# Loading, casting and transposing the first batch in two parts, with neighbouring heads paired and its keys evicted straight into blocks

## Chip, cores and metric

One core of one Trainium2 chip. The metric is the device time of one execution in microseconds, as the median of several runs. Engines: PE (TensorE, matrix products and transposes), DVE (VectorE), ACT (ScalarE), POOL (GpSimd), SP (issues most loads). In the profile L12 is line 12 of that kernel's source; line numbers differ from kernel to kernel.

## The reference

Sliding-window attention (8 batches, 8 heads, 576 positions, head size 64, window 32), followed by a two-layer network on all 4608 tokens.

```python
scores = scale * q @ k.T                        # (8, 8, 576, 576), kept where |i - j| <= 32
attn = softmax(scores)
x = (attn @ v).transpose(0, 2, 1, 3).reshape(4608, 512)
h = x @ w_in                                    # w_in 512 x 2048
out = np.maximum(0.01 * h, h) @ w_out           # w_out 2048 x 512, float32 out
```

## The kernel before

Heads are worked on in pairs, four to a batch. Each (batch, half of the sequence, pair) is one *attention step*: `score(i)` (five matmuls `ps`, exponential `e` on ACT, mask product `pr` on POOL) and `weighted(i)` (row sums `s`, weighted values `x`, reciprocal `r` and product `xT` on DVE). Four steps fill 288 rows of `xT`. These feed 16 *h tiles* (one h group), and every 128 rows of `gT` give one *output tile*.

```python
def load_qk(b, p, behind=None):
    for into, src, name in ((qf, q, "qf"), (kf, k, "kf")):
        t = fload.tile([96, 2, RUN * D], FP32, name=f"{name}{p}")
        if behind is not None:                      # the marker: a copy of 4 bytes that waits
            nc.sync.dma_start(out=t[0:1, 0, 0:1], in_=behind.bitcast(FP32))
            behind = None
        nc.sync.dma_start(out=t, in_=src[b, p:H:NPAIR].rearrange(...))   # heads p and p+4
...
# transposes(b): per pair q and k, 6 transposes each into one PSUM tile, then
nc.scalar.activation(out=kT_v, in_=tok, func=AF.Copy)
for a in range(2):
    nc.vector.tensor_copy(out=kbd[b % 2][r, p, :, r], in_=kT[r]...)      # keys into diagonal blocks
...
def o_tile(j, hook=None):
    o = mmps.tile([128, 512], FP32, name="mm", tag="mm")
    for f in range(FFC):
        if hook and f % 4 == 0:
            hook()                                  # steps that are due are put in here
        nc.tensor.matmul(o, gT[...], w_out_bf[:, f, :], ...)
    o_sb = outp.tile([128, DMODEL], FP32, name="o_sb")
    nc.scalar.activation(out=o_sb, in_=o, func=AF.Copy)
    nc.scalar.dma_start(out=out[ts(j, 128), :], in_=o_sb)
...
for i in range(NPAIR):                              # the start: steps 0 to 3
    score(i + 1)
    ...
    if i < 2: load_w_in(1024 + 512 * i, 1536 + 512 * i)
    else:     load_w_out(i - 2)
    weighted(i)
for p in range(NPAIR):                              # batch 1's q and k, behind a w_in chunk
    load_qk(1, p, w_in_bf[0:1, 0, 512:514] if p == 0 else None)
step(); load_w_out(2); load_w_out(3)
for f in range(FFC):                                # first h group, steps 5 to 7 in it
    h_tile(0, f)
    if f in (2, 6, 10): step()
    ...
for p in range(NPAIR):                              # batch 1's v, behind a w_out chunk
    load_v(1, p, w_out_bf[0:1, 4, 0:2] if p == 0 else None)
for f in range(FFC):                                # second h group, batch 1's transposes in it
    h_tile(1, f)
    if f % 4 == 3: next(second); next(second); ...
score(8)
# from here: output tiles with steps 8 to 11, third h group, and so on
```

The schedule is manual: each engine executes its instructions in the order written here.

The softmax here doesn't subtract the row's maximum and nothing guards it: scores larger than these inputs give would overflow.

## Time and profile before

| kernel before | us |
|---|---|
| time, median of 3 runs | 350.79 (350.40 to 351.71) |
| span of the profiled run | 349.3 |
| TensorE busy | 324.9 |
| first h tile starts | 28.91 |
| third h group starts | 70.37 |

The prediction below shows the lines of the start, the first h group and the first output tiles. Two more stretches complete the table of stages. The columns are the stretch, its length, busy time of PE, PEld, DVE, ACT and POOL with counts, granted clock, DMA share and GB/s.

```profile
41.55:52.25 10.70, 10.70 (x118) 8.49 (x116) 5.19 (x10) 9.73 (x24) 6.68 (x8) 1.00 0.91 193
70.37:349.30 278.93, 270.39 (x2285) 184.00 (x2301) 145.18 (x152) 162.27 (x355) 129.18 (x147) 1.00 0.34 96
```

The second h group has no idle PE time at all, and the rest of the kernel (279 us) is 97% busy.

### The profile page before, as it was taken

Reading aid. Unit: us, or ns where it says so; the run is one execution under the profiler, and the core shown is the slowest. Engines: PE = TensorE matmul, PEld = TensorE weight load, DVE = VectorE, ACT = ScalarE, POOL = GpSimd, SP = SyncE. Lnnn points to the kernel's source line nnn. Section 1 sums busy time; section 2 is a strip of 40 time slices with the busy share of each in tenths; the row PEclk is TensorE's granted clock in tenths of the full one; section 3 lists DMA queues with packets and bytes.
Section 4 is the critical chain, followed back from the end, with each engine's and each line's share of the span. In section 5 each row is a group of like instructions: output and inputs, shape, how many; then the busy total and the mean of one; then the engine's idle time right before and its main releaser. Section 6 shows DMA issues by size and latency. Waiting matters only on the chain.

```text
span 349.3 us, 6917 instructions
## 1 busy us (share of the span) xinstructions
PE 324.9 (93%) x2731; PEld 221.3 (63%) x2752; DVE 189.2 (54%) x206; ACT 203.8 (58%) x431; POOL 179.1 (51%) x213
## 2 busy tenths in 40 slices
PE   2558999998899999999999999999999999999995
PEld 1346775585675767667675766667675766666652
DVE  5487833865446656466456656566356656555200
ACT  6763793385563856566564756567474756455441
POOL 7696767566745636555354636555264644222000
PEclk9999999999999999999999999999999999999999
DMA  8999989968754433543444433553301001010101
GB/s 185 208 197 227 269 174 240 261 135 228 168 137 130 134 98 107 142 149 69 127 130 136 134 84 100 145 169 70 111 19 62 30 2 62 0 63 0 62 17 73
DMA packets 60708, 42.39 MB, mean 121 GB/s; under 512 B 39684, under 2 KB 56068, under 8 KB 60676
## 3 DMA queue, kind: packets, MB, share of 16 engines
q1 hardware_dynamic: 51204, 28.32, 34.7%
q10 hardware_dynamic: 5184, 9.44, 7.4%
q0 software_dynamic: 4288, 4.20, 7.3%
q8 instruction: 21, 0.34, 0.4%
q14 instruction: 11, 0.09, 0.1%
HBM read 36.70 MB, written 9.44 MB: 132 GB/s over the span
## 4 chain that ended last, share of the span: by engine, by line
PE 82%; ACT 5%; DVE 3%; issue 2%; DMA 2%; SPq 2%; POOL 1%; ACTq 1%; DVEq 0%; POOLq 0%
PE mm L280 35%; PE mm L266 33%; PE x L247 4%; PE tp L188 3%; PE ps L221 3%; DVE r L253 2%; DMA kf<-in_k_dram 2%; PE s L239 2%; ACT o_sb L285 2%; PE s L240 2%; ACT gT L270 1%; SPq L81 1%; SPq L70 1%; ACTq L286 1%; ACT kT L202 1%
## 5 line engine op out<-in xcount | busy, mean ns | idle before, releaser
L253 DVE RECIPROCAL r<-s 128x288 f32<-128x288 f32 x64 | 125.3, 1958 | 92.2 <-PE s L240 91.9
L231 POOL TENSOR_TENSOR pr<-e,mask 128x544 bf16<-128x544 bf16 x64 | 77.7, 1214 | 130.5 <-ACT e L227 130.3
L266 PE MATMUL mm<-xT,w_in_bf 128*128 128x288 bf16 x1024 | 136.8, 288 | 1.5 <-ACT gT L270 1.5
L280 PE MATMUL mm<-w_out_bf,gT 128*128 128x512 bf16 x555 | 128.1, 379 | 1.1
L266 PEld LDWEIGHTS <-w_in_bf 128*128 128x128 bf16 x1024 | 98.8, 98 | 28.7 <-issue 3.2
L270 ACT ACTIVATE gT<-mm 128x288 bf16<-128x288 f32 x256 | 101.9, 413 | 23.0 <-PE mm L266 8.8
L280 PEld LDWEIGHTS <-gT 128*128 128x128 bf16 x576 | 55.3, 98 | 60.5
L285 ACT ACTIVATE o_sb<-mm 128x512 f32<-128x512 f32 x36 | 21.5, 597 | 85.6 <-PE mm L280 85.6
L227 ACT ACTIVATE e<-ps 128x544 bf16<-128x544 f32 x64 | 39.8, 622 | 24.1 <-PE ps L221 12.9
L205 DVE COPY kbd<-kT 64x576 bf16<-64x576 bf16 x64 | 28.4, 444 | 32.4 <-ACT kT L202 32.0
L176 POOL CAST vbd<-vf 64x576 bf16<-64x576 f32 x58 | 38.4, 661 | 2.3 <-DMA vf<-in_v_dram 0.4
L255 DVE TENSOR_TENSOR xT<-x,r 128x288 bf16<-128x288 f32 x64 | 29.3, 458 | 6.7
L166 POOL CAST kb<-kf 96x768 bf16<-96x768 f32 x32 | 26.7, 837 | 8.1 <-DMA kf<-in_k_dram 8.1
L221 PE MATMUL ps<-qT,kbd 128*128 128x128 bf16 (+2 forms) x320 | 27.6, 220 | 0.0
L247 PE MATMUL x<-pr,vbd 128*128 128x128 bf16 (+2 forms) x320 | 27.1, 218 | 0.4 <-DVE xT L255 0.2
L221 PEld LDWEIGHTS <-kbd 128*128 128x128 bf16 x320 | 21.3, 103 | 7.2
L247 PEld LDWEIGHTS <-vbd 128*128 128x128 bf16 x320 | 21.8, 102 | 4.7 <-issue 1.9
L202 ACT ACTIVATE kT<-tp 128x576 bf16<-128x576 bf16 x32 | 20.8, 651 | 4.6 <-PE tp L188 2.8
L239 PE MATMUL s<-pr,ones_bd 128*128 128x288 bf16 x64 | 19.1, 298 | 4.7 <-DVE r L253 3.3
L196 ACT ACTIVATE qT<-tp 128x576 bf16<-128x576 bf16 x32 | 20.7, 648 | 3.9 <-PE tp L188 3.1
L188 PE MATMUL tp<-ident,qb 96*128 96x96 bf16 x192 | 14.4, 214 | 8.2 <-DVE qb L166 6.4
L166 POOL CAST qb<-qf 96x768 bf16<-96x768 f32 x24 | 19.7, 819 | 0.0
(31 smaller groups left out, 107.8 us busy)
## 6 DMA issues: line engine op xcount, KB each, us to landing
qf<-in_q_dram SPq DMA_DIRECT2D x32, 288.0 KB, 3.8
kf<-in_k_dram SPq DMA_DIRECT2D x32, 288.0 KB, 4.1
vf<-in_v_dram SPq DMA_DIRECT2D x64, 144.0 KB, 3.7
out_dram<-o_sb ACTq DMA_DIRECT2D x36, 256.0 KB, 2.3
w_in_bf<-in_moe_w_in_dram POOLq DMA_DIRECT2D x8, 256.0 KB, 6.4
w_out_bf<-in_moe_w_out_dram POOLq DMA_DIRECT2D x4, 512.0 KB, 12.8
qf<-w_in_bf SPq DMA_DIRECT2D x1, 0.0 KB
vf<-w_out_bf SPq DMA_DIRECT2D x1, 0.0 KB
```

The source lines that it names most:

```text
L166: eng.tensor_copy(out=dst[:, p], in_=src[b, p].rearrange("p a (c d) -> p c a d", d=D),)
L176: nc.gpsimd.tensor_copy(out=vbd[b % 2][r, p, :, r], in_=vf[b, p][r])
L221: nc.tensor.matmul(ps[:, c0:c0 + n], kbd[b % 2][:, p, blk], qT[b][:, p, q0:q0 + n], start=True, stop=True,)
L227: nc.scalar.activation(out=e, in_=ps[:, 512 - HALF:512 - HALF + NCOL], func=AF.Exp, scale=scale,)
L231: nc.gpsimd.tensor_mul(pr, e, mask[hf])
L247: nc.tensor.matmul(x[:, a:a + n], vbd[b % 2][:, p, blk, :], pr[:, c0:c0 + n], start=(n_ == 0), stop=(n_ == len(WIN[hf]) - 1), skip_group_c ...
L253: nc.vector.reciprocal(r, s)
L255: nc.vector.tensor_mul(xT[:, p, t0:t0 + HALF], x, r)
L266: nc.tensor.matmul(h[:, 0:HALF], w_in_bf[:, c, ts(f, 128)], xT[:, c, ds(t0, HALF)], start=(c == 0), stop=(c == DMC - 1),)
L270: nc.scalar.activation(out=gT[:, f, ds(t0, HALF)], in_=h[:, 0:HALF], func=AF.Prelu, alpha=0.01,)
L280: nc.tensor.matmul(o, gT[:, f, ds(128 * j % RING, 128)], w_out_bf[:, f, :], start=(f == 0), stop=(f == FFC - 1),)
L285: nc.scalar.activation(out=o_sb, in_=o, func=AF.Copy)
```

## The change

It is meant to shorten the start. Batch 0's q, k and v arrive in two parts by sequence, so that steps 0 to 3, which need only the first half of the queries, can begin before the rest is loaded, cast and transposed. Heads 2p and 2p+1 are paired in place of p and p+4, so a pair lies together in memory. Batch 0's keys go from PSUM straight into the blocks, without the DVE copies. To make room, other work moves: the second parts' casts and transposes and steps 4 to 7 into the first h group, two tiles apart; w_out's loads behind step 7; batch 1's loads behind w_out; batch 1's transposes and score 8 into the output tiles.

```diff
-                out=t, in_=src[b, p:H:NPAIR].rearrange("a (p c) d -> p a (c d)", c=RUN),
+                out=t, in_=src[b, 2 * p:2 * p + 2].rearrange("a (p c) d -> p a (c d)", c=RUN),
...
+    PART_Q = ((0, 3), (HALF, 3))
+    PART_K = ((0, 4), (384, 2))
+    PART_V = ((0, 5), (5, NB))
...        (load_qk0, load_v0, cast_qk0, cast_v0, transposes0: the same work for one part)
+                        kbd[0][r, p, t0 // 64:t0 // 64 + 96 * run // 64, r].rearrange(
+                            "p n (i c) -> p n i c", c=run),
+                        in_=tp[r].rearrange("p c (n i) -> p n i c", i=64 // run), func=AF.Copy,
...
-    for p in range(NPAIR):
-        load_qk(1, p, w_in_bf[0:1, 0, 512:514] if p == 0 else None)
-    step()
-    load_w_out(2)
-    load_w_out(3)
+    transposes0(0, 1)
+    score(4)
+    cast_v0(0, 1)
     for f in range(FFC):
         h_tile(0, f)
-        if f in (2, 6, 10):
-            step()
+        if f % 2 == 1:
+            i = (f - 1) // 2
+            if i < 3:
+                cast_qk0(i + 1, 1)
+                cast_v0(i + 1, 1)
+                transposes0(i + 1, 1)
+            if 1 <= i < 5:
+                step()
+            if i >= 4:
+                load_w_out(i - 4)
...
+        load_qk(1, p, w_out_bf[0:1, 4, 0:2] if p == 0 else None)
...
+    def step1():
+        i = state["done"]
+        if i == 8:
+            cast_v(1, 0)
+            score(8)
+        if i < 11:
+            cast_v(1, i - 7, on_act=i % 2 == 0)
+        load_v(2, i - 8)
+        step()
+    due += [(O_US * (3.9 + 2 * p), transposes1) for p in range(NPAIR)]
+    due += [(O_US * (8.9 + 1.6 * p), step1) for p in range(NPAIR)]
```

More of the change, by code (lines that the diff above doesn't have):

```diff
@@ L82, in load_v, with columns, load_qk0, load_v0 @@
                 out=t[64 * a:64 * a + 64],
-                in_=v[b, NPAIR * a + p].rearrange("(c p) d -> p c d", p=64),
+                in_=v[b, 2 * p + a].rearrange("(c p) d -> p c d", p=64),
             )
         vf[b, p] = t
-    load_qk(0, 0)
-    load_qk(0, 1)
-    load_v(0, 0)
-    load_qk(0, 2)
-    load_v(0, 1)
-    load_qk(0, 3)
-    load_v(0, 2)
-    load_v(0, 3)
+    PART_Q = ((0, 3), (HALF, 3))
+    PART_K = ((0, 4), (384, 2))
+    PART_V = ((0, 5), (5, NB))
+    for p in range(NPAIR):
+        qf[0, p] = fload.tile([96, 2, RUN * D], FP32, name=f"qf{p}")
+        kf[0, p] = fload.tile([96, 2, RUN * D], FP32, name=f"kf{p}")
+        vf[0, p] = fload.tile([128, NB, D], FP32, name=f"vf{p}")
+    def columns(part):
+        t0, run = part
+        return t0 // 96, t0 // 96 + run
+    def load_qk0(p, h):
+        for t, src, part in ((qf[0, p], q, PART_Q[h]), (kf[0, p], k, PART_K[h])):
+            t0, run = part
+            c0, c1 = columns(part)
+            nc.sync.dma_start(
+                out=t[:, :, c0 * D:c1 * D],
+                in_=src[0, 2 * p:2 * p + 2, t0:t0 + 96 * run].rearrange(
+                    "a (p c) d -> p a (c d)", c=run),
+            )
+    def load_v0(p, h):
+        n0, n1 = PART_V[h]
+        for a in range(2):
+            nc.sync.dma_start(
+                out=vf[0, p][64 * a:64 * a + 64, n0:n1],
+                in_=v[0, 2 * p + a, 64 * n0:64 * n1].rearrange("(c p) d -> p c d", p=64),
+            )
+    for p in range(NPAIR + 1):
+        if p < NPAIR:
+            load_qk0(p, 0)
+        if p > 0:
+            load_v0(p - 1, 0)
+    for p in range(NPAIR):
+        load_qk0(p, 1)
+        load_v0(p, 1)
     ident_f = const.tile([128, 128], FP32)
@@ L120, in clear @@
         )
-    nc.vector.memset(kbd[0], 0.0)
-    clear(vbd[0], 0)
-    clear(vbd[0], 1)
+    nc.vector.memset(kbd[0][:, 0:2], 0.0)
+    for p in range(3):
+        clear(vbd[0], p)
     WIN = [
@@ L147, with make_mask @@
     mask = [const.tile([128, NCOL], BF16, name=f"mask{i}") for i in range(2)]
-    def make_masks():
-        for hf in range(2):
-            lo = W * (hf + 1)
-            nc.gpsimd.tensor_copy(out=mask[hf][:, 0:HALF], in_=win_f[:, lo:lo + HALF])
-            nc.gpsimd.tensor_copy(out=mask[hf][:, HALF:NCOL], in_=win_f[:, 0:NCOL - HALF])
+    def make_mask(hf):
+        lo = W * (hf + 1)
+        nc.gpsimd.tensor_copy(out=mask[hf][:, 0:HALF], in_=win_f[:, lo:lo + HALF])
+        nc.gpsimd.tensor_copy(out=mask[hf][:, HALF:NCOL], in_=win_f[:, 0:NCOL - HALF])
     RING = 4 * HALF
@@ L176, in cast_v, with cast_qk0, cast_v0, transposes0 @@
                 nc.gpsimd.tensor_copy(out=vbd[b % 2][r, p, :, r], in_=vf[b, p][r])
+    def cast_qk0(p, h):
+        for eng, src, dst, part in (
+            (nc.vector, qf, qb, PART_Q[h]), (nc.gpsimd, kf, kb, PART_K[h]),
+        ):
+            c0, c1 = columns(part)
+            eng.tensor_copy(
+                out=dst[:, p, c0:c1],
+                in_=src[0, p][:, :, c0 * D:c1 * D].rearrange("p a (c d) -> p c a d", d=D),
+            )
+    def cast_v0(p, h, on_act=False):
+        n0, n1 = PART_V[h]
+        for a in range(2):
+            r = slice(64 * a, 64 * a + 64)
+            to, src = vbd[0][r, p, n0:n1, r], vf[0, p][r, n0:n1]
+            if on_act:
+                nc.scalar.activation(out=to, in_=src, func=AF.Copy)
+            else:
+                nc.gpsimd.tensor_copy(out=to, in_=src)
+    def transposes0(p, h):
+        if 0 not in qT:
+            qT[0] = attn.tile([128, NPAIR, S], BF16, name="qT")
+        for src, part in ((qb, PART_Q[h]), (kb, PART_K[h])):
+            t0, run = part
+            c0, c1 = columns(part)
+            tp = mmps.tile([128, run, 96], BF16, name="tp0", tag="mm")
+            for c in range(run):
+                nc.tensor.transpose(
+                    tp[:, c], src[:, p, c0 + c].rearrange("p a d -> p (a d)"), ident[0:96, 0:96],
+                )
+            if src is qb:
+                nc.scalar.activation(
+                    out=qT[0][:, p, t0:t0 + 96 * run].rearrange("p (i c) -> p i c", c=run),
+                    in_=tp.rearrange("p c i -> p i c"), func=AF.Copy,
+                )
+            else:
+                for a in range(2):
+                    r = slice(64 * a, 64 * a + 64)
+                    nc.scalar.activation(
+                        out=kbd[0][r, p, t0 // 64:t0 // 64 + 96 * run // 64, r].rearrange(
+                            "p n (i c) -> p n i c", c=run),
+                        in_=tp[r].rearrange("p c (n i) -> p n i c", i=64 // run), func=AF.Copy,
+                    )
     def transposes(b, first=False):
@@ L333, in step, with load_w_in @@
         state["done"] += 1
-    w_in_r = moe_w_in.rearrange("(a u d) f -> a d u f", a=2, d=D)
+    w_in_r = moe_w_in.rearrange("(u r) f -> r u f", r=128)
     w_out_r = moe_w_out.rearrange("(c p) f -> p c f", p=128)
-    def load_w_in(f0, f1):
-        for a in range(2):
-            nc.gpsimd.dma_start(
-                out=w_in_bf[64 * a:64 * a + 64, :, f0:f1], in_=w_in_r[a, :, :, f0:f1],
-            )
+    def load_w_in(i):
+        f = slice(512 * i, 512 * i + 512)
+        nc.gpsimd.dma_start(out=w_in_bf[:, :, f], in_=w_in_r[:, :, f])
     def load_w_out(i):
@@ L347, in load_w_out @@
         nc.gpsimd.dma_start(out=w_out_bf[:, c, :], in_=w_out_r[:, c, :])
-    first = transposes(0, first=True)
-    def first_pair():
-        next(first)
-        next(first)
-    cast_qk(0, 0, nc.vector)
-    make_masks()
-    cast_qk(0, 1, nc.vector)
-    first_pair()
-    first_pair()
-    clear(vbd[0], 2)
-    cast_v(0, 0)
-    cast_qk(0, 2, nc.vector)
-    score(0)
-    load_w_in(0, 512)
-    first_pair()
-    clear(vbd[0], 3)
-    cast_qk(0, 3, nc.vector)
-    load_w_in(512, 1024)
-    for i in range(NPAIR):
-        score(i + 1)
-        if i + 1 < NPAIR:
-            cast_v(0, i + 1, on_act=True)
-        if i < 2:
-            load_w_in(1024 + 512 * i, 1536 + 512 * i)
-        else:
-            load_w_out(i - 2)
-        weighted(i)
-        if i == 0:
-            first_pair()
@@ L380 @@
-    state["done"] = NPAIR
-    for p in range(NPAIR):
-        load_qk(1, p, w_in_bf[0:1, 0, 512:514] if p == 0 else None)
-    step()
-    load_w_out(2)
-    load_w_out(3)
+    cast_qk0(0, 0)
+    make_mask(0)
+    nc.vector.memset(kbd[0][:, 2:4], 0.0)
+    cast_qk0(1, 0)
+    nc.vector.memset(vbd[0][:, 3], 0.0)
+    transposes0(0, 0)
+    transposes0(1, 0)
+    cast_v0(0, 0)
+    cast_qk0(2, 0)
+    score(0)
+    transposes0(2, 0)
+    score(1)
+    cast_v0(1, 0, on_act=True)
+    cast_qk0(3, 0)
@@ L389 @@
+    weighted(0)
+    load_w_in(0)
+    transposes0(3, 0)
+    score(2)
+    cast_v0(2, 0, on_act=True)
+    weighted(1)
+    load_w_in(1)
+    score(3)
+    cast_v0(3, 0, on_act=True)
+    make_mask(1)
+    load_w_in(2)
+    weighted(2)
+    cast_qk0(0, 1)
+    load_w_in(3)
+    weighted(3)
+    state["done"] = NPAIR
+    transposes0(0, 1)
+    score(4)
+    cast_v0(0, 1)
     for f in range(FFC):
         h_tile(0, f)
-        if f in (2, 6, 10):
-            step()
-        if f % 4 == 3:
-            nc.gpsimd.memset(kbd[1][:, f // 4], 0.0)
+        if f % 2 == 1:
[8 more added lines that the diff above has]
+                load_w_out(i - 4)
@@ L395 @@
     for p in range(NPAIR):
-        cast_qk(1, p, nc.vector)
+        load_qk(1, p, w_out_bf[0:1, 4, 0:2] if p == 0 else None)
     for p in range(NPAIR):
-        load_v(1, p, w_out_bf[0:1, 4, 0:2] if p == 0 else None)
-    second = transposes(1, first=True)
+        load_v(1, p)
     for f in range(FFC):
@@ L402 @@
         if f % 4 == 3:
-            next(second)
-            next(second)
+            nc.gpsimd.memset(kbd[1][:, f // 4], 0.0)
             nc.gpsimd.memset(vbd[1][:, f // 4], 0.0)
+    for p in range(NPAIR):
+        cast_qk(1, p, nc.vector)
+        load_qk(2, p)
+    second = transposes(1, first=True)
     state["tp"] = 16
-    score(8)
-    for p in range(NPAIR):
-        load_qk(2, p)
     H_US, O_US, LEAD = 4 * (HALF / 2400 + 2.5e-3), 4 * 0.216, 4.0
@@ L428, with transposes1 @@
     due = []
-    for i in range(8, NC):
-        prev = 0.9 * O_US * 4 if i < 12 else at[i // 4 - 1] - LEAD
-        due.append(prev + (at[i // 4] - LEAD + (1.2 if i < 12 else 0) - prev) * (i % 4 + 1) / 4)
+    for i in range(12, NC):
+        g = i // 4
+        due.append((at[g - 1] + (at[g] - at[g - 1]) * (i % 4 + 1) / 4 - LEAD, step))
+    def transposes1():
+        next(second)
+        next(second)
+    def step1():
[9 more added lines that the diff above has]
+    due += [(O_US * (8.9 + 1.6 * p), step1) for p in range(NPAIR)]
+    due.sort(key=lambda t: t[0])
     clock = 0.0
-    cast_v(1, 0)
-    load_v(2, 0)
     def spend(us):
         nonlocal clock
-        while due and due[0] <= clock:
-            due.pop(0)
-            i = state["done"]
-            if i < 11:
-                cast_v(1, i - 7)
-                load_v(2, i - 7)
-            step()
+        while due and due[0][0] <= clock:
+            due.pop(0)[1]()
         clock += us
```

## The prediction

> **What bounds the kernel now.** I read the page first (busy shares), then the busy times by stretch, then TensorE's timeline, the groups of instructions, the DMA view and the SyncE queue's timeline.
>
> ```profile
> PE 324.9 (93%) x2731; PEld 221.3 (63%) x2752; DVE 189.2 (54%) x206; ACT 203.8 (58%) x431; POOL 179.1 (51%) x213
> ```
> TensorE is busy for 324.9 of 349.3 us, so 24 us is all that a reordering can win. Where they lie is told by the stretches: before the first h tile (28.9), the first h group with attention steps 4 to 7 (to 41.55), the second (to 52.25), the first output tiles (to 70.37).
>
> ```profile
> 0.00:28.90 28.90, 13.43 (x113) 9.57 (x114) 18.27 (x27) 18.13 (x25) 23.17 (x38) 1.00 1.12 197
> 28.90:41.55 12.65, 12.50 (x99) 9.39 (x98) 9.79 (x9) 7.29 (x17) 8.62 (x9) 1.00 1.17 256
> 52.25:70.37 18.12, 17.86 (x127) 9.87 (x127) 10.76 (x11) 6.34 (x11) 11.41 (x14) 1.00 1.19 249
> ```
> The columns are length, busy PE, PEld, DVE, ACT, POOL, granted clock, DMA share, GB/s. TensorE is idle for 15.5 us of the first 28.9, and for only 0.15 and 0.26 us in the two others. So the change can win at the start alone, and in the later stages it can only lose. DMA is full in all three.
>
> ```profile
> 25.26 0.42 PE L239 MATMUL s<-pr,ones_bd 128*128 128x288 bf16 x1 [1.06 <-DVE r L253]
> 27.95 0.42 PE L239 MATMUL s<-pr,ones_bd 128*128 128x288 bf16 x1 [1.06 <-DVE r L253]
> 28.91 3.08 PE L266 MATMUL mm<-xT,w_in_bf 128*128 128x288 bf16 x12
> 33.15 2.45 PE L266 MATMUL mm<-xT,w_in_bf 128*128 128x288 bf16 x16
> ```
> The start ends in a chain of steps 2.69 us apart (25.26 to 27.95): each sum s waits for the reciprocal before it, as s and x have one buffer. Then come h tiles, 12 matmuls in 2.9 us (0.24 each) at first, later 16 in 2.2 (0.14).
>
> ```profile
> L253 DVE RECIPROCAL r<-s 128x288 f32<-128x288 f32 x64 | 125.3, 1958 | 92.2 <-PE s L240 91.9
> L231 POOL TENSOR_TENSOR pr<-e,mask 128x544 bf16<-128x544 bf16 x64 | 77.7, 1214 | 130.5 <-ACT e L227 130.3
> ```
> A step costs 1.96 us of reciprocal plus 0.46 of multiply on DVE, and 1.21 on POOL. I use both below.
>
> ```profile
> 23.03 0.72 SPq L68 DMA_DIRECT2D qf<-w_in_bf  x1
> 27.54 0.34 SPq L70 DMA_DIRECT2D qf<-in_q_dram  x1
> 38.24 0.62 SPq L79 DMA_DIRECT2D vf<-w_out_bf  x1
> 46.39 0.68 SPq L81 DMA_DIRECT2D vf<-in_v_dram  x1
> ```
> Batch 1's loads are held back by one-element marker copies, which wait for a weight chunk. From the first marker's issue to the next load passed 4.5 us. Batch 1's v was all in near 54-55, only 2 to 3 us after the first output tile.
>
> **What the Trainium skill says.** "TensorE: Matmul & The Clock Gate", What's actually happening: TensorE idles at 1.2 GHz and gets 2.4 after about 3.4 us of sustained work. The trace agrees: 0.24 us per 288-column matmul up to 33, then about 0.14, though the page's clock row says 1.00 throughout. An earlier start of h therefore runs its first 4 to 5 us at half rate as before. "DMA: Bandwidth & Descriptors", Specifications: at least 512 B is needed for line rate. The trace agrees: packets under 512 B (v alone, 48 to 52 us) moved at 196 GB/s, those of q and k (55 to 60) at 261. Halved q and k runs keep to 512 B or more. The same page, Queues, rings and completion order: each engine takes queues in turn, a packet at a time. That fits the marker's 4.5 us beside weight loads, though no view shows the turn itself.
>
> **Rates and durations.** From the DMA view by stretch: v 3141 packets in 4 us on 16 engines, 20 ns a packet; q and k 907 in 5 us, 88 ns; weights 1216 in 6 us, 79 ns. So w_in and w_out (2048 packets each) are 10.1 us each, batch 1's q and k (1536) 8.5, its v (4608) 5.9. ACT reads 576 columns in 0.65 us and 288 in 0.41, so I estimate 0.49 for 384 and 0.34 for 192. POOL's cast of 768 takes 0.82, so 0.55 for 512 and 0.30 for 256 (estimates).
>
> **The change, part by part.**
>
> 1. *Half loads.* By the same rates the first parts make about 2.3 us of DMA per pair, where whole pairs made 3.8. kb of pair 3 was cast at 16.63; its half should land near 11.5. Data then no longer holds the start.
>
> 2. *Straight eviction.* Eight DVE copies of 0.44 us go, and ACT makes two evictions of 0.49 where it had one of 0.65. So DVE is freed and ACT is level.
>
> 3. *The start, walked through the new order of each engine.* ACT clears three blocks to 5.6, evicts pair 0 to 7.1 and pair 1 to 8.5, then exp to 9.1. POOL casts k2 to 9.4, pr0 to 10.6, pr1 to 12.75 and, queued behind it, k3 to 13.3. Sums: s0 at 10.65; s1 at 14.4 (behind k3's transposes); s2 at 17.05 and s3 at 19.7, both behind the reciprocal. Then follow transposes of pair 0's second part and score 4 (22.95). First h tile at **23.0 against 28.9: 5.9 us won**.
>
> 4. *The first h group.* It takes 12.65 us now. New in it: 15 transposes (0.65 us at full rate, more while cold) and waits. TensorE waits about 0.6 us for k1's cast behind pr4 and v0's casts on POOL; 1.45 us for q3's cast, which DVE has in line behind the reciprocal and multiply of step 4; and 1.75 us in steps 6 and 7, as these stand 2 h tiles apart (1.1 us and 0.75 of attention) while a reciprocal and multiply need 2.5. Before, four tiles stood between steps. That is 3.8 us of waits, 1.5 of transposes, 1.2 more at half rate: 19.1 in place of 12.65. It ends near 42.1, against 41.55. **The 5.9 us are given back here.** DVE meanwhile idles from 22.5 to 29.6, for step 4 comes only after four h tiles.
>
> 5. *The second h group* loses batch 1's 48 transposes (2.0 us) and score 8 (0.24): 16 tiles of 0.553, to 50.95 against 52.25. This work only moves into the output tiles, which now hold 18.1 + 2.3 = 20.4. Without waits the third h group would start at 71.4, against 70.4.
>
> 6. *Batch 1's data.* w_out is now issued behind pr7 (37.2), no longer at 24.6; DMA has finished w_in near 31 and idles. First packets at about 39.5, second chunk landed near 45.3, marker, q and k issued near 50, v0 landed near 62. The last w_out chunk lands near 50.5, in time. Batch 1's transposes are ordered from 54 on, 2.2 us apart, as its k lands (54.3, then 2.1 apart): waits of about 1 us. Step 8 is reached near 61.6, but pr8 is in POOL's line behind v0's casts: 62.2 + 1.4 + 1.2 = 64.8. A wait of 3.2 us; then steps at the reciprocal's pace keep 1 us more. The third h group starts near 75.7, **5.3 us late**.
>
> After that both orders are the same and TensorE-bound (270.4 of the last 278.9 us busy). Walked result: 350.8 + 5.3 = 356.
>
> **The rivals.** *Rival A, the start's gain survives.* If the first h group runs with no new waits, the third group starts near 71.4 - 3.8 = 67.6, and if batch 1 also comes in time the kernel takes about 348. For it: fewer DVE copies, and transpose times that fit k's landing so well that they look tuned. Against: 2.5 us of DVE per step against 1.85 of work between. *Rival B, only the batch 1 wait is smaller.* The marker may take 2 us in place of 4.5, as less is queued; packets may start 1 us sooner. Then step 8 waits next to nothing and the result is about 352. *Rival C, transfers collide at the start:* w_in shares DMA with second parts, chunk 0 is issued at 13.3 and lands only near 22, so the first h tile has 1 us of margin; POOL being 2 us late would make it 358.
>
> **Range and chances.** My walk took the slow value for the marker (2.5 us spread) and for TensorE's clock (cold to 29; 1.2 us spread). Half of both, 1.9, comes off 356: **354 us**. Each stage of the walk may be off by 1 to 2 us and three add up, so 347 to 359.5. Faster by over 2% (under 343.8) needs the 5.9 us kept and one more: 5%. Slower by over 2% (over 357.8) needs the walk and some of rival C: 16%. Within 2%: 79%.
>
> **What would show it.** First h matmul near 23 (within 1.5 us); the stretch from there to the second h group 17 to 20 us long, with TensorE waiting for qb behind DVE and for r; w_out issued after 35, DMA share falling between 31 and 39; q and k of batch 1 issued near 50; step 8's sum waiting for pr; third h group at 73 to 76. After it nothing should change: the length from there to the end is 279 us in both. I am wrong if the h stage shows no waits for DVE, if batch 1's v lands before the steps ask for it, or if the later stages shift by more than 1 us.

## More of the kernel before

One more stretch, cut by time, is needed to compare DMA later:

```profile
30.00:40.00 10.00, 9.85 (x81) 7.43 (x80) 7.24 (x7) 6.04 (x14) 5.97 (x7) 1.00 1.16 260
```

## The result and the profile after

The changed kernel takes **360.5 us** (359.86 to 360.62, 4 runs) beside 350.7 for the kernel before: ratio 1.027, 95% interval 1.0247 to 1.0294, so slower. A ratio here is the mean time of one kernel's fast runs over that of the other's fast runs of the same rounds, so not quite the ratio of the medians quoted. Outputs are correct.

The busy times by stretch of the changed kernel, cut at the same events (start, first h tile, second h group, first output tile, third h group, end):

```profile
0.00:21.84 21.84, 10.81 (x86) 7.30 (x87) 14.83 (x20) 15.76 (x29) 16.08 (x30) 1.00 0.85 180
21.84:41.50 19.66, 14.64 (x125) 10.78 (x124) 11.43 (x12) 11.01 (x28) 13.97 (x22) 1.00 0.70 116
41.50:49.33 7.83, 7.83 (x67) 6.25 (x65) 0.00 (x0) 6.57 (x17) 5.97 (x6) 1.00 1.17 189
49.33:79.66 30.33, 24.63 (x180) 13.66 (x177) 15.60 (x21) 13.54 (x23) 11.91 (x13) 0.89 1.01 215
79.66:358.80 279.14, 271.44 (x2307) 184.13 (x2303) 145.02 (x152) 162.65 (x355) 129.34 (x147) 1.00 0.37 101
```

| stage | before, us | after, us | difference | predicted for after |
|---|---|---|---|---|
| start | 28.91 | 21.84 | -7.07 | 23.0 |
| first h group | 12.64 | 19.66 | +7.02 | 19.1 |
| second h group | 10.70 | 7.83 | -2.87 | 8.85 |
| first output tiles | 18.12 | 30.33 | +12.21 | 24.75 |
| rest | 278.93 | 279.14 | +0.21 | 279 |

The last column's 24.75 is the prediction's 75.7 less its 50.95. The start gains 7.1 us and the first h group gives all of it back. The first output tiles lose 12.2 us; the second h group, whose transposes and score moved there, gains 2.9. What is left, 9.3 us, is the whole loss.

TensorE's timeline in the first h group (start, busy time, group; in brackets the idle time before it and what ended it):

```profile
25.44 0.34 PE L239 MATMUL tp<-ident,kb 96*128 96x96 bf16 x2 [1.23 <-POOL kb L215]
31.96 0.30 PE L239 MATMUL tp<-ident,qb 96*128 96x96 bf16 x3 [1.85 <-DVE qb L215]
35.31 0.28 PE L317 MATMUL s<-pr,ones_bd 128*128 128x288 bf16 x1 [0.96 <-POOL pr L309]
37.75 0.30 PE L317 MATMUL s<-pr,ones_bd 128*128 128x288 bf16 x1 [0.83 <-DVE r L331]
```

Each second part's transposes wait for a cast that stands in its engine's line behind an attention step, and steps 6 and 7 wait for their own predecessors: these four waits are 4.9 us of idle time, in a stage that had 0.15.

Now the data of batch 1. The same stretch by time as before:

```profile
30.00:40.00 10.00, 6.21 (x65) 4.74 (x65) 8.37 (x8) 4.72 (x13) 8.03 (x11) 1.00 0.22 34
```

34 GB/s in place of 260: DMA has next to nothing to do, because w_out is issued by POOL only behind step 7's mask product, and batch 1 waits behind w_out. POOL's timeline (issue of w_out; a cast of v0 and step 8's mask product), then SP's queue:

```profile
36.37 3.03 POOL L423 DMA_DIRECT2D w_out_bf<-in_moe_w_out_dram  x4
...
63.89 0.67 POOL L207 CAST vbd<-vf 64x576 bf16<-64x576 f32 x1 [0.15 <-DMA vf<-in_v_dram]
64.64 1.21 POOL L309 TENSOR_TENSOR pr<-e,mask 128x544 bf16<-128x544 bf16 x1
```
```profile
45.46 0.72 SPq L68 DMA_DIRECT2D qf<-w_out_bf  x1
49.82 0.34 SPq L70 DMA_DIRECT2D qf<-in_q_dram  x1
```

Batch 1's q starts at 49.82 (before: 27.54), and its v0 is cast at 63.89. TensorE's timeline in the first output tiles shows the waits that follow:

```profile
53.84 0.43 PE L266 MATMUL tp<-ident,qb 96*128 96x96 bf16 x6 [0.89 <-DVE qb L197]
55.21 0.43 PE L266 MATMUL tp<-ident,kb 96*128 96x96 bf16 x6 [0.95 <-POOL kb L197]
55.48 3.16 PE L358 MATMUL mm<-w_out_bf,gT 128*128 128x512 bf16 x8
...
64.08 0.40 PE L299 MATMUL ps<-qT,kbd 128*128 128x96 bf16 x5 [0.86 <-ACT e L305]
65.90 0.28 PE L317 MATMUL s<-pr,ones_bd 128*128 128x288 bf16 x1 [1.42 <-POOL pr L309]
```

Waits are not all. The eight matmuls at 55.48 take 3.16 us, where eight elsewhere take 1.89. The stretches around them, with the granted clock in the third column from the right:

```profile
53.00:55.50 2.50, 0.72 (x13) 0.58 (x14) 0.56 (x1) 1.23 (x2) 0.82 (x1) 1.00 1.05 246
55.50:59.40 3.90, 3.90 (x25) 1.98 (x22) 1.11 (x2) 0.89 (x2) 0.83 (x1) 0.56 1.09 242
...
62.80:66.10 3.30, 1.02 (x13) 0.77 (x12) 1.21 (x3) 2.61 (x6) 2.75 (x4) 1.00 1.30 229
66.10:70.25 4.15, 4.15 (x27) 2.43 (x26) 2.42 (x3) 1.80 (x3) 2.48 (x3) 0.59 1.22 205
```

Twice TensorE was busy for less than a third of a stretch (0.72 of 2.50, 1.02 of 3.30), and the granted clock in the next four microseconds was 0.56 and 0.59. Little activity is not enough for this: in e1 below TensorE was busy for 0.68 of 2.50 us (60.75 to 63.25), in e9 it idled for 2.81 us in one piece (up to 58.19), and the clock stayed at 1.00 both times. The lost clock is 3.90 x 0.44 + 4.15 x 0.41 = 3.4 us. This fits the Trainium skill, "TensorE: Matmul & The Clock Gate", What's actually happening: the clock is either full or half and follows recent activity. (Granted over 56 to 58 us in this trace: 0.50.)

### The profile page after: what moved, and what is told of

It reads as the page before. It is cut to its first block, busy times and chain, and to the rows that moved or that the text cites. A ratio compares the mean times of both kernels' runs of the same rounds, so it can differ in the third digit from the quotient of the medians.

```text
span 358.8 us, 6975 instructions
## 1 busy us (share of the span) xinstructions
PE 329.3 (92%) x2752; PEld 222.1 (62%) x2752; DVE 186.9 (52%) x204; ACT 209.5 (58%) x450; POOL 177.3 (49%) x217
## 4 chain that ended last, share of the span: by engine, by line
PE 72%; DMA 9%; ACT 6%; SPq 4%; issue 3%; POOL 2%; DVE 2%; ACTq 1%; POOLq 0%; DVEq 0%
PE mm L358 32%; PE mm L344 28%; DMA vf<-in_v_dram 4%; PE x L325 3%; PE tp L266 3%; PE ps L299 3%; SPq L114 2%; DMA w_out_bf<-in_moe_w_out_dram 2%; ACT o_sb L363 2%; SPq L105 2%; PE s L317 2%; DMA qf<-in_q_dram 1%; POOL pr L309 1%; PE s L318 1%; DMA qf<-w_out_bf 1%
## 5 line engine op out<-in xcount | busy, mean ns | idle before, releaser
L358 PE MATMUL mm<-w_out_bf,gT 128*128 128x512 bf16 x576 | 133.1, 384 | 0.2 <-ACT o_sb L363 0.2
L283 DVE COPY kbd<-kT 64x576 bf16<-64x576 bf16 x56 | 24.9, 444 | 24.4 <-ACT kT L280 24.0
L207 POOL CAST vbd<-vf 64x576 bf16<-64x576 f32 x52 | 34.4, 662 | 2.2 <-DMA vf<-in_v_dram 0.6
L197 POOL CAST kb<-kf 96x768 bf16<-96x768 f32 x28 | 23.1, 826 | 12.3 <-DMA kf<-in_k_dram 12.3
L274 ACT ACTIVATE qT<-tp 128x576 bf16<-128x576 bf16 x28 | 18.2, 649 | 8.0 <-PE tp L266 5.7
L280 ACT ACTIVATE kT<-tp 128x576 bf16<-128x576 bf16 x28 | 18.2, 650 | 2.6 <-PE x L325 1.4
L318 PE MATMUL s<-pr,ones_bd 128*128 128x256 bf16 x64 | 18.0, 282 | 0.0
```

What stands on the lines that cost most here:

```text
L197: eng.tensor_copy(out=dst[:, p], in_=src[b, p].rearrange("p a (c d) -> p c a d", d=D),)
L207: nc.gpsimd.tensor_copy(out=vbd[b % 2][r, p, :, r], in_=vf[b, p][r])
L358: nc.tensor.matmul(o, gT[:, f, ds(128 * j % RING, 128)], w_out_bf[:, f, :], start=(f == 0), stop=(f == FFC - 1),)
```

## The experiments

Sixteen runs were made (e11 repeats e8's kernel), all with correct outputs. Quoted ratios are to the kernel before on the same chip, whose median was 350.6 to 352.0 us. "Third group" is the start of the third h group in the profile (70.37 before, 79.66 after), which says when the stages concerned are over.

**Theories.** T1: batch 1's late data is what costs the 9.3 us. Rivals: T2, the marker's latency; T3, the half clock by itself; T4, the first h group's end; T5, the pairing of neighbours; and, later, T6, the output stores that hold ACT, and T7, the steps' own order.

### Data early, and data late

**e1: w_out's loads early, in the changed kernel.** The marker lets batch 1 follow w_out, so this moves all loads.

```diff
     load_w_in(3)
+    load_w_out(0)
+    load_w_out(1)
...              transposes0(i + 1, 1)
+                if i == 1:
+                    load_w_out(2)
+                    load_w_out(3)
-            if i >= 4:
-                load_w_out(i - 4)
```

> The changed kernel, with w_out's four loads issued among the first h group's work (two after w_in's last, two after the casts of pair 2) in place of behind the last mask multiply of the group. Theory (batch 1's data comes late because w_out's issue and the marker behind it come late): w_out's issues move from 36.4-39.4 us to about 21-29, batch 1's q and k from 49.8 to about 41, no wait for qb, kb or pr in the first output tiles, granted clock 1.00 there, third h group near 70 in place of 79.7, total about 351 (349.5 to 353). The first h group stays as it is or is 1 us longer (POOL issues ahead of k1's cast). Rival (the waits inside the first h group are what costs): those waits stay, so the total stays near 360.

Measured: 355.88 us, ratio 1.0145 (1.0124 to 1.0166), third group 75.13. Batch 1's q starts at 40.02. The output tiles of this run:

```profile
49.46:75.13 25.67, 21.29 (x180) 12.21 (x178) 14.41 (x19) 13.38 (x23) 10.30 (x11) 1.00 1.17 225
```

The clock is back at 1.00 and the third group is 4.5 us sooner: about half of the loss. The stage is 4.66 us shorter; 3.0 us of that lie before step 8's sum, which now comes 13.56 us into the stage and not 16.57, and 1.65 after it, where the clock makes the difference (see e3). But the expected 351 is missed by 5 us, and 4.4 us of idle time stay.

**e7: the opposite, the kernel before with late loads** (w_out issued in the first h group behind tile 6, batch 1's q and k behind its second chunk; batch 1's v loses its own marker, as in the change).

```diff
-        else:
-            load_w_out(i - 2)
...
+        if f == 6:
+            for i in range(4):
+                load_w_out(i)
+            for p in range(NPAIR):
+                load_qk(1, p, w_out_bf[0:1, 4, 0:2] if p == 0 else None)
```

> The kernel before with one thing of the change alone: w_out is issued behind the last mask multiply of the first h group (36.6 us) and batch 1's q and k behind w_out's second chunk. Theory of late data: q and k go out near 49 to 50 in place of 27.5; here batch 1's transposes stand in the second h group, from 43 on, so TensorE waits for kb there, 8 us or more in all; total 358 to 363. If late loads were harmless (hidden by the output tiles): within 2 us of 350.8.

Measured: 364.94 us, ratio 1.0363 (1.0318 to 1.0408), a little over the range. TensorE's timeline of this run:

```profile
55.32 0.66 PE L188 MATMUL tp<-ident,qb 96*128 96x96 bf16 x6 [11.96 <-DVE qb L166]
```

Late loads alone cost as much as the whole change, with nothing else of it present. That there are 11.96 us in one wait is due to the order of this kernel, which has batch 1's transposes in the second h group; so the direction is shown here, and not the changed kernel's size. (The changed kernel moved these transposes back, which suits the late data.)

**e2: no marker at all** (q and k of batch 1 issued at once).

```diff
-        load_qk(1, p, w_out_bf[0:1, 4, 0:2] if p == 0 else None)
+        load_qk(1, p, None)
```

> The changed kernel without the marker copy, so batch 1's q and k go out as soon as their buffers are free (about 23 to 32 us), in the gap in which DMA idles. Theory of late data: batch 1 is there before the output tiles ask for it; w_out still starts at 36-38 and now shares DMA with batch 1's tail, so the first output tile may wait 1 to 2 us for its last chunk. Third h group near 71-72, total 351 to 354. Rival (the marker is not what delays, POOL's and DVE's own queues are): still waits of 4 us or more in the first output tiles, total above 357.

Measured: 361.98 us with one slow run among the four (fast ones 358.75 to 363.25), ratio 1.0253 of the fast runs (1.0213 to 1.0294): no clear gain, expectation missed. In the profiled run, the slowest of the fast ones, TensorE now waits for the weights in the first output tile, 1.19 us at 52.64 and then

```profile
56.15 1.86 PE L358 MATMUL mm<-w_out_bf,gT 128*128 128x512 bf16 x4 [2.48 <-DMA w_out_bf<-in_moe_w_out_dram]
```

The marker does order two loads that are both needed by then, and removing it only swaps which comes late. e1 keeps the marker and gains, so w_out's place behind step 7 is a fault by itself. The marker's latency alone (4.4 us) was not tested: that part of T2 stays open.

### The clock

**e3: idle transposes in the output tiles, to keep TensorE's clock up.** The text says 78 of them; the edit made 186 (18 before each of eight transposes, 18 and 24 at step 8), 186 x 0.0425 = 7.9 us of extra work (in the timelines 12 transposes take 0.51 us). e10 repeats it with 78.

```diff
+    def warm(n):
+        tp = tps.tile([128, RUN, 96], BF16, name="tp")
+        for c in range(n):
+            nc.tensor.transpose(tp[:, c % RUN], ident[0:96, :], ident[0:96, 0:96])
...
+        warm(18)
         next(second)
```

> The changed kernel with 78 idle transposes of a constant put where TensorE waits in the first output tiles (18 before each transpose of batch 1 and before score 9, 24 before step 8's sum); they carry no data. It separates the slow clock from the waits. If the slow clock (0.56 and 0.59 in two stretches of 4 us) is a cost of its own: granted clock 1.00 in the first output tiles, and 1.5 to 3.5 us faster, 357 to 359, though the waits for data stay; the first of the two dips should win little, as step 8 waits for pr until 65.9 anyway. If the slow clock costs nothing beside the waits: 360.5 or up to 3 us more.

> e3_filler held 186 idle transposes (18 before each of batch 1's eight, 18 and 24 at step 8), not 78 as its text said: 7.9 us of TensorE work that cost only 1 us in all. Here 78: 18 before each of pair 0's two transposes, 18 before score 9, 24 before step 8's sum, so 3.3 us laid where TensorE waits. If the slow clock is a cost of its own: granted clock 1.00 in the output tiles and 1 to 3.5 us faster than the changed kernel (357 to 359.5 where the kernel before has 350.7). If it is only a companion of the waits: equal to the changed kernel or slower.

Measured: e3 361.51 us (ratio 1.0305), e10 361.49 us (1.0274, that of the changed kernel). The output tiles of e3:

```profile
49.68:80.49 30.81, 28.94 (x365) 20.04 (x363) 15.60 (x21) 13.96 (x23) 11.90 (x13) 1.00 1.10 237
```

The clock is 1.00 there, and the stage is as long as before: 7.9 us of needless work cost only about 1 us, and full clock seems to give nothing. But the filler stands in the slow stretches too, so this is no fair test of T3. The piece from step 8's sum to score 10 shows it; here are its end in the changed kernel (it begins at 65.90, above), then both ends in e1 and in e3:

```profile
70.25 0.40 PE L299 MATMUL ps<-qT,kbd 128*128 128x96 bf16 x5
...
63.02 0.28 PE L317 MATMUL s<-pr,ones_bd 128*128 128x288 bf16 x1 [0.96 <-POOL pr L309]
65.73 0.40 PE L299 MATMUL ps<-qT,kbd 128*128 128x96 bf16 x5
...
66.83 0.28 PE L317 MATMUL s<-pr,ones_bd 128*128 128x288 bf16 x1 [0.23 <-POOL pr L309]
71.07 0.40 PE L299 MATMUL ps<-qT,kbd 128*128 128x96 bf16 x5
```

TensorE is busy throughout. The changed kernel takes 4.35 us at a granted clock of 0.61, e1 2.71 us for the same instructions at 1.00, and e3 4.24 us at 1.00, for it has 36 idle transposes (1.5 us) in this piece: they took what the clock gave back. (e2, e4 and e10 have the piece at 0.61 as well and take 4.33 to 4.37 us.) From score 10 to the third h group the changed kernel takes 9.41 us and e1 9.40. So the 1.64 us of this slow stretch are passed on in full. The first slow stretch (55.5 to 59.4) is another matter: step 8's sum waits until 65.90 for v0's landing, cast and mask product, whatever TensorE does before, so it cost nothing here. T3 is thus right for about half of the lost clock, 1.6 of the 9.3 us. The dips came with late data: all four timed executions of the changed kernel have a mean clock of 0.99 to 0.995, three of e1's four have 1.00 and the fourth 0.995. What exactly sets one off, the runs do not show. In e10 the clock was 0.94 from 49.3 to 80 us, slow in this same piece, so that run does not settle it.

### The first h group

**e4: steps 4 to 7 after tiles 3, 7, 10 and 13; q3's cast ahead of step 4's reciprocal.**

```diff
-            if 1 <= i < 5:
-                step()
+        if f in (3, 7, 10, 13):
+            step()
+        if f % 2 == 1 and f >= 9:
+            load_w_out((f - 9) // 2)
```

> The changed kernel with steps 4 to 7 of the first h group spread over it (after tiles 3, 7, 10 and 13, in place of 3, 5, 7 and 9) and q3's cast ahead of step 4's reciprocal on DVE. Theory of late data: the waits in the first h group (4.8 us of idle TensorE) fall to about 1, its end moves from 41.5 to about 38, but w_out still goes out behind the last mask multiply, near 35.5, so batch 1 comes less than 1 us sooner and the total stays at 359.5 to 360.5. Rival (the first h group's waits are what costs): 3 to 3.5 us faster, 357.

Measured: 358.3 us, ratio 1.0212. The first output tile starts 1.1 us sooner (48.23). But the third group is 2.7 us sooner (76.94), about as much as batch 1's loads are (47.21 for 49.82): my edit had let w_out slip ahead of step 7. That confound makes it a weak test of T4, though the third group moved with the loads and not with the h group.

**e5 and e6: e1's early loads, with batch 1's transposes and score 8 sooner and its steps two quarters of an output tile apart (e5); e6 also has the first h group reordered.**

```diff
-    due += [(O_US * (3.9 + 2 * p), transposes1) for p in range(NPAIR)]
-    due += [(O_US * (8.9 + 1.6 * p), step1) for p in range(NPAIR)]
+    due += [(O_US * (0.9 + 2 * p), transposes1) for p in range(NPAIR)]
+    due += [(O_US * 3.9, score8)]
+    due += [(O_US * (7.9 + 2 * p), step1) for p in range(NPAIR)]
```

> e1_wout_early plus the steps of batch 1 spread over the output tiles: transposes at 0.9, 2.9, 4.9 and 6.9 quarter tiles, score 8 at 3.9 ahead of v0's cast on POOL, steps at 7.9, 9.9, 11.9 and 13.9 (they stood at 3.9 to 9.9 and 8.9 to 13.7, with scores 8 and 9 back to back). In e1_wout_early 4.4 us of TensorE idle are left in the first output tiles though the data is there (0.86 for exp between the two scores, 0.96 and 0.77 for pr, 0.49 for r, 0.52 for qT). If these are the steps' own spacing, they fall below 1.5 us: third h group near 71 to 72, total about 352. If they come from data or from POOL's other work, the total stays at 355 to 356.

> e5_spread plus a first h group in another order: v0's second cast ahead of pr4 on POOL, step 4's sum after the second h tile and ahead of pair 1's transposes, steps 5 to 7 after tiles 5, 8 and 11, all casts of q ahead of the reciprocal they waited behind. If the waits of the first h group cost only once the data is early, this is where they show: its 19.7 us fall to 16 to 17, and the total is 2 to 3.5 us below e5_spread, 348 to 350, so faster than the kernel before. If the first h group is off the path even now, the same as e5_spread.

Measured: e5 354.35 us (ratio 1.0064, third group 73.82), e6 354.05 us (1.005, 74.94). e5 misses its expectation by some 2 us. e6 reaches its first output tile 2.1 us before e5 (47.27) and ends no sooner (its profiled run is the slowest of its four), for it then waits 1.96 us for a DVE copy behind casts whose data is not there yet. An earlier h group is worth nothing as long as batch 1's path sets the next stage, so T4 is not what cost here. e6 does not show it cleanly, though: its trace also has the hold that e9 explains below (first output tile complete at 52.55, its store issued at 56.08, ACT idle for 4.02 us). And once the holds are gone the earlier h groups do count: e16 below begins its output tiles at 46.62, 2.7 us before the changed kernel, and keeps that.

### What held ACT

**e9: e6's order, loads of batch 1 behind a w_in chunk, casts of v on POOL.**

```diff
-        load_qk(1, p, w_out_bf[0:1, 4, 0:2] if p == 0 else None)
+        load_qk(1, p, w_in_bf[0:1, 0, 1024:1026] if p == 0 else None)
```

> A version meant to keep the early start: the changed kernel with the first h group and the steps ordered as in e6_rework and k3's cast ahead of w_out's last issues on POOL, w_out issued early, batch 1's q and k let go by a chunk of w_in (as in the kernel before) so they share DMA with w_out, and v1 to v3 of batch 1 cast on POOL. If late loads and the places of the steps are the whole loss: no wait for DMA or kbd in the output tiles, first output tile near 45.5, third h group near 68.5, 1.5 to 2.5 us faster than the kernel before. If the early start cannot be kept because DMA is full until about 54 in either order: third h group at 70 to 72, equal to the kernel before or slower.

Measured: 353.97 us, ratio 1.0071 (1.0036 to 1.0106), third group 73.14 in place of 68.5. Batch 1's q now starts at 33.62, 16 us before that of the changed kernel, so a late q and k can't be what is left. ACT's timeline and queue in this run:

```profile
51.34 0.60 ACT L363 ACTIVATE o_sb<-mm 128x512 f32<-128x512 f32 x1
56.49 0.38 ACTq L364 DMA_DIRECT2D out_dram<-o_sb  x1
56.97 0.62 ACT L305 ACTIVATE e<-ps 128x544 bf16<-128x544 f32 x1 [5.04 <-DMA vf<-in_v_dram]
```

The tile `o_sb` is complete at 51.94, but its store is issued at 56.49, and the exponential of step 8 stands behind it for 5.04 us. It has no use for v. The list of waits of the built program (from building this run's kernel, not from the trace) tells what the store waits for:

```
ACT   DMACopy out_dram<-o_sb                    waits DMAHW6, Activation
SP    DMACopy vf<-in_v_dram (pair 2, 2nd head)  waits DMAHW6
```

Transfers issued by ACT and by SP take turns on eight completion semaphores in this program (DMAHW0 to DMAHW7). The store's turn falls on one that a load of batch 1's v still holds, so it waits for that landing, and ACT's line with it. In the kernel before, the first store (56.53) follows its `o_sb` (55.90 + 0.60) at once; the transfer that its turn fell on was evidently done.

**e12: e9 with the stores of the first four tiles issued by POOL** (in the built program they wait on another set of semaphores). **e13** and **e14** make that move alone in the changed kernel and in e5; **e15** in e8 (below).

```diff
-        nc.scalar.dma_start(out=out[ts(j, 128), :], in_=o_sb)
+        (nc.gpsimd if j < 4 else nc.scalar).dma_start(out=out[ts(j, 128), :], in_=o_sb)
```

> The reordered kernel with early data (the one called best before), with the output stores of the first four tiles issued by POOL instead of ACT. Theory, the first store holds ACT (5.04 us before one exponential) and with it the transposes and steps of batch 1: ACT waits for no landing behind a store, the third h group starts near 69 in place of 73.1 and the kernel takes about 349. Rival, the steps' own order and POOL's casts set the stage: third h group stays at 72 to 73, 353 to 354.

> The changed kernel with only that move of the stores. Theory, k and v of batch 1 land at 54 to 64 there and hold the stage anyway: at most 2 us faster than the changed kernel's 360.5, third h group 77.5 to 79.7. Rival, the store is the main cause in the changed kernel too: 355 or less, third h group near 74.

> The kernel with w_out early and the steps spread out, with that move of the stores. Theory: third h group near 71.5 to 72 in place of 73.8, kernel 351.5 to 352.5 beside a before of 350.8 to 352. Rival, steps' order: unchanged, ratio 1.006.

Measured: e12 350.52 us, ratio 0.998 (0.9954 to 1.0007), third group 69.58, 3.6 us sooner than e9's with the start equal (first h tile 22.30 in both). ACT's timeline in e12:

```profile
51.44 0.60 ACT L363 ACTIVATE o_sb<-mm 128x512 f32<-128x512 f32 x1
52.45 0.62 ACT L305 ACTIVATE e<-ps 128x544 bf16<-128x544 f32 x1 [0.41 <-PE ps L299]
```

The exponential comes 4.5 us earlier. T6 holds for this order. e13: 362.33 us, ratio 1.0306, third group 79.75: no gain, as expected, since q, k and v arrive from 54 to 64 there and the store (0.8 us late) is hidden behind them. e14: 354.26 us, ratio 1.0085, as e5: expectation missed. Its ACT timeline shows no store, but casts of v (60.26 to 61.65) ahead of the exponential at 61.67. Its output tiles are 1.4 us shorter than e5's (23.11 for 24.49 us), while its first h tile came 0.9 us later, in a part that the edit does not touch. This suggests that T6 and T7 are both at work, and that it depends on the order which of two holds on ACT counts.

**e16: e12 with the casts of v2 and v3 (and batch 2's load of v) behind the step instead of ahead of it** (in e12 one sum waited 1.62 us for a mask product behind such a cast on POOL).

```diff
     def step1():
         i = state["done"]
-        if i in (8, 9):
-            cast_v(1, i - 6)
-        load_v(2, i - 8)
         step()
+        if i in (8, 9):
+            cast_v(1, i - 6)
+        load_v(2, i - 8)
```

> The reordered kernel with stores on POOL (350.5, third h group 69.58), with the casts of batch 1's v2 and v3 placed behind the step's score instead of ahead of it. In that run pr10 started at 59.88 behind a cast of 1.38 us and the sum behind it waited 1.62 us. Theory, POOL's line is what is left: the wait falls to about 0.3, third h group near 68.2, 349 to 349.5, ratio to before 0.993 to 0.995. Rival, DVE's reciprocal pace holds the steps anyway (2.4 us a step beside tiles of 1.73): no change, 350.5, 0.998.

Measured: 349.35 us (6 runs), ratio 0.9955 (0.9938 to 0.9972), third group 67.92; the longest wait of a sum in the output tiles is 0.49 us. Its output tiles as a stretch:

```profile
46.62:67.92 21.30, 20.37 (x180) 11.97 (x178) 14.50 (x19) 10.58 (x20) 14.65 (x18) 1.00 1.18 234
```

21.30 us where the changed kernel takes 30.33 for the same work. The expectation is met but for the wait (0.49 for about 0.3), and the reordered kernel now gains over the kernel before, if only by half a per cent, as much as e8 and e11 below do without the reordering.

### The pairing alone

**e8: the kernel before, with neighbouring heads paired and w_in loaded in one transfer a chunk. e11 repeats it with five rounds; e15 adds the stores on POOL.**

```diff
-                out=t, in_=src[b, p:H:NPAIR].rearrange("a (p c) d -> p a (c d)", c=RUN),
+                out=t, in_=src[b, 2 * p:2 * p + 2].rearrange("a (p c) d -> p a (c d)", c=RUN),
...
-    w_in_r = moe_w_in.rearrange("(a u d) f -> a d u f", a=2, d=D)
+    w_in_r = moe_w_in.rearrange("(u r) f -> r u f", r=128)
```

> The kernel before with neighbour pairing alone: heads 2p and 2p+1 in a pair, w_in's rows to match and its load in one transfer of 128 partitions in place of two of 64. Runs and packets are of the same sizes, POOL issues 4 transfers fewer. All theories: the same within 0.5 us (350.3 to 351.2); if it moves more, part of the change's cost or gain is here.

> e8_pairs_in_before again, as its ratio (0.9934, 0.9893 to 0.9975) came on a chip where the kernel before scattered by 3 us. If neighbour pairing with one load of w_in per chunk is a gain, a ratio of 0.993 to 0.998 with an interval below 1; if the scatter made it, 1.000 within 0.002.

> The kernel before with neighbour pairs (ratio 0.995), with the stores of the first four tiles on POOL. There TensorE idles only about 0.3 us in the first output tiles, so both theories expect no change: ratio 0.993 to 0.997. If it gets slower, POOL's issuing of a store[...] costs something by itself, and the runs above carry that cost too.

Measured: e8 349.78 us (0.9934, 0.9893 to 0.9975), e11 349.82 us (0.9952, 0.9918 to 0.9986), e15 350.25 us (0.9971, 0.9943 to 0.9999). T5 falls: the pairing, with the single load of a w_in chunk that is in the same edit, costs nothing and gains about half a per cent. e15 shows no gain from moving stores where ACT is not held.

## Why the prediction was wrong

The direction was the likelier of its two losing sides, and the time lies outside its range: 360.5 for 354 (347 to 359.5). By its own steps:

1. *Steps 1 to 3, half loads, straight eviction, start:* right in kind. First h tile at 21.84 against 23.0; the gain is 7.1 us, not 5.9.
2. *Step 4, the first h group:* right, 19.66 for 19.1, "the 5.9 us are given back here". The waits named are the waits seen (k's cast on POOL, q3's cast on DVE, steps 6 and 7), with 4.9 us for 3.8. That the total is so close is partly luck: about 1.1 us more idle time (5.0 in all) and 0.6 us less work (14.64 busy) than it summed. Rival A is refuted by the same lines.
3. *Step 5, the second h group:* right in kind; its 16 tiles took 0.49 us each and not 0.553, so output tiles began at 49.33 for 50.95.
4. *Step 6, batch 1's data:* **this is the step that failed, by size.** Every event in it came as told: w_out at 36.4 (37.2), q and k issued at 49.8 (near 50), v0 landed just before its cast at 63.9 (62), step 8's sum at 65.9 behind POOL (64.8). But it put the third group at 75.7, "5.3 us late", and it came at 79.66, 9.3 us late. Of the 4.0 us between, 1.1 had gathered by step 8's sum and 2.9 came after it (13.76 us to the third group, where the prediction had 75.7 - 64.8 = 10.9). The largest part of the 2.9 is the half clock: 1.64 us, by the piece that e1 runs in 2.71 us and the changed kernel in 4.35. The prediction quoted the rule of the clock for the start, but took the work of the output tiles at full clock: 20.4 us, where TensorE was busy for 24.63 (e1 21.29, e16 20.37). Another 0.9 us is a slip in its sum: the waits that step 6 lists, 1 + 3.2 + 1, are 5.2 us (5.70 were measured), and 71.4 + 5.2 is 76.6, not 75.7. The remaining 0.3 or so is not assigned.
5. *Where the 9.3 us come from:* e1 shows that early w_out and batch 1 return 4.7 us of the stage, 3.0 before step 8's sum and 1.65 through the clock after it. The reordered kernels show the rest in ACT's and POOL's lines (in the start of the third group, e9 to e12 3.6 us, e12 to e16 1.7 us). These were found in kernels with early data. That in the changed kernel itself the same holds stand behind the late data, each ready to take its place, is what e1, e5 and e13 suggest together, but no run measures their shares there.
6. *After the third group* nothing changes: 279.14 for 278.93, as predicted.
7. *Range:* the walk gave 356, and 1.9 us were taken off for having used slow values. Both took their slow values: the marker (45.46 to 49.82), and TensorE's clock in the first h group (eight matmuls took 2.13 us from 21.84 on, and 1.14 us only from 28.96). So taking half of them off was wrong in direction. Without it, the walk less the 1.6 us won before the output tiles plus the 5.6 lost in them is 360. Rival B is refuted by the same marker. Rival C's collision was not seen: the first h tile was not held by w_in.

## What to carry to other kernels

A reordering that frees one stage has to be followed through the issue times of the *next* loads: here w_out was tied to step 7 and batch 1 to w_out, and ten microseconds of nearly idle DMA (34 GB/s) cost 4.7 us in the next stage (e1). When a stage waits on data and on a chain of short steps over four engines, look at each engine's line for something that does not need to be there (a store, a cast for a later step), because one hold removed shows the next. And where idle time and a slow clock appear together, compare the same instructions with a run that has no dip (here 4.35 us for 2.71), and ask what waits for them: one slow stretch cost its full 1.6 us, the other lay beside a wait for data and cost nothing. Filler cannot tell this if it stands in the slow stretch itself.

## What the Trainium skill lacked or had wrong

- "DMA: Bandwidth & Descriptors", Issuing engines are not separate DMA queues, says that starting transfers from several engines saves only sequencer time, usually small. For the transfer that may be so. But the choice of engine decided here whose line a store could hold: ScalarE stood 5.04 us behind one store, and moving four stores to another engine's queue took the kernel from 1.0071 to 0.998 of the time before (some 3.2 us). No page that I read tells that a kernel's transfers can share completion semaphores in turn, so that a store waits for an unrelated load.
- "TensorE: Matmul & The Clock Gate", HAM oscillation — how this bites in real kernels, gives as the rule no idle gaps above about 3.4 us. Here no gap in the two stretches ahead of the slow ones was above 1.42 us; TensorE was busy for 0.72 of 2.50 us and for 1.02 of 3.30 us, and the clock that followed was 0.56 and 0.59. The page mentions short idle times between groups as another way to lose the clock, but not how little activity is too little; nor do these runs tell it, as 0.68 us of 2.50 in e1 and a gap of 2.81 us in e9 left the clock at 1.00. What the page says of two states agrees with the granted clock of 0.50 over 56 to 58 us, and with eight matmuls that took 3.16 us there for 1.89.
- "DMA: Bandwidth & Descriptors", Latency and other measured facts, speaks of a fixed cost of about 2 us a transfer. From the issue of a marker of 4 bytes to the next load it was 45.46 to 49.82, 4.4 us, beside weight loads (3.6 us in e1, 4.6 in e9).
